# Unread matmuls in the gaps of the first attention steps, and three v loads split by rows

## The chip, the cores and the metric

The kernel runs on one core of a Trainium2 chip. Its time is the device time of one execution in microseconds (us). The timed runs are three; the profile is of one further execution. Engines are named as in the profile: PE (TensorE), PEld (its weight loads), DVE (VectorE), ACT (ScalarE), POOL (GpSimd) and SP, whose queue issues all the DMAs.

## The reference

Three stages follow each other. Attention over q, k, v of shape (2, 8, 576, 64), where a query sees only 32 keys: heads 0 to 3 the last 32 positions ("plain"), heads 4 to 7 every fourth of the last 128 ("dilated"). Then a layer with a softmax gate and a layer norm (512 to 1024 to 512). Then four experts, each 512 to 1024 with a ReLU and back, summed with the weights of each token.

```
masks = plain: 0 <= rel < 32;  dilated: 0 <= rel < 128 and rel % 4 == 0
attn  = softmax(where(mask, q @ k.T / 8, -1e9));  x = attn @ v
h     = x @ w_in;  solu = h * softmax(h);  x = layernorm(solu) * g @ w_out
out   = sum over e of p[:, e] * (relu(x @ w1[e]) @ w2[e])
```

Every output element depends on all of these. Nothing in the reference uses the products of the tile `warm`.

## The kernel before, in words

Attention is cut into 12 units: quad "P" (plain heads) and "D" (dilated heads), three tiles t each, for two batches b. A unit, `att_U`, has twelve steps: (1) score matmuls on PE, two that write the mask (line 256) and 24 small ones on q and k (line 265, 48 records in the profile); (2) the maximum on DVE (line 273); (3) subtraction on DVE (275); (4) exp on ACT (278); (5) sum (280) and (6) reciprocal (282) on DVE; (7) the product pd (284); (8) three transposes on PE (289); (9) copy to pt; (10) value matmuls on PE on pt and v (300); (11) copy to xhi; (12) the remainder xlo on DVE (238). PSUM tiles of the pool "pa" alternate between two buffers, so a unit's PE step can also wait for a DVE or ACT step of an earlier unit.

Beside it the weights of the first layer, in 64-bit floats, are converted: `conv_in` (VI.j) takes a loaded tile draw through ACT (lines 180, 182), DVE (184, 186), an addition (188), a copy to wh and a remainder wl (213). The first layer's matmuls `moe_H` (H.t, line 330) need the xhi and xlo of their tokens and wh and wl. Each matrix product is made of three products of high and low parts.

The order of all this is written out by hand in the string ORDER, one word per step: `UP.1.0` is the next step of unit P, t = 1, b = 0; `VI.2` the next of conversion 2; `lP`, `lD`, `lI`, `lvp`, `lvd`, `lO` issue a load; `F.n` calls `warm_up(n)`. A "+" chooses another engine for steps that have a choice. Each engine runs its share of that order strictly in sequence, and the SP queue issues loads in that order.

`warm_up(n)` issues n matmuls of 128x512 bf16 on a constant tile of ones into a PSUM tile that nobody reads. There are 16 in ORDER: `F.10` ahead of everything, then `F.2`, `F.1`, `F.1` and `F.2` between attention steps.

A load of v is one DMA of 128 rows of 3072 bytes: `load_vp(u, b)` takes a tile from a pool of two buffers, `load_vd(c, b)` fills a tile of its own. In SP's order of the opening, `lvp.0.0`, `lvd.1.0` and `lvd.0.0` come first, then `lP.0.1`, `lvp.1.0`, `lvp.2.0` (which takes the buffer that `lvp.0.0` filled, so it waits until unit P.0.0 has used it), `lI.3` (the draw load of conversion 3), `lD.1.1`, `lD.0.1`, `lvd.2.0`, and `lO.0.0`.

Of the kernel before, what the change touches and what calls it, by code (L numbers as in the profile page):

```python
# [23 lines left out]

ORDER = """
lP.0.0+ F.10 UP.0.0+ lI.0 lD.0.0 UD.0.0 UP.0.0 UP.0.0 VI.0 VI.0 VI.0+ VI.0+ UD.0.0+ UD.0.0 VI.0+ UP.0.0 UP.0.0 lI.4 VI.4+ VI.4 VI.4 VI.4+ VI.0 VI.4+ lD.1.0
UD.0.0 UD.0.0+ UD.0.0+ UD.0.0+ VI.4 F.2 UD.1.0 UD.1.0+ UP.0.0+ UP.0.0+ UD.1.0 lP.1.0+ VI.4+ VI.0+ F.1 UP.1.0 UP.1.0+ UD.1.0 UD.1.0 UD.1.0+ UD.1.0+ UP.1.0+
UP.1.0+ UD.2.0 UD.2.0 UD.2.0 UP.0.0 F.1 UP.2.0+ UP.0.0+ lI.1+ lI.2+ VI.1+ VI.1+ lO.0.1 VI.2+ UP.1.0+ UP.1.0+ UP.1.0+ UD.1.0 UD.1.0 UP.2.0+ UP.2.0+ VI.2
lvp.0.0 lvd.1.0 VI.1 F.2 UP.0.0 VI.1+ VI.1+ lvd.0.0 lP.0.1+ UP.0.0 UP.0.0+ UP.2.0+ UP.2.0+ UD.1.0 UD.1.0 UD.1.0+ VI.2 VI.2+ UD.0.0+ UD.0.0 VI.1 lvp.1.0 H.0+
UP.1.0+ VI.2+ lvp.2.0 VI.1 UP.0.1+ UP.1.0 UD.0.0 UP.0.1+ UP.0.1+ UP.2.0+ H.0 UD.2.0+ UD.2.0+ UD.2.0 UD.0.0 UD.0.0 lI.3 VI.3 UP.1.0+ UP.1.0 lD.1.1 UP.1.0  # L30
UD.2.0 VI.3+ VI.3 VI.3+ VI.2 H.1 VI.3 UD.2.0 lD.0.1 UD.0.1+ lvd.2.0+ UD.2.0 H.1+ UD.2.0+ VI.2 UD.0.1+ UD.0.1 UP.2.0+ VI.3 H.0 UP.0.1 UP.0.1+ UD.2.0 VI.3+
UD.2.0 UP.0.1+ UD.1.1+ UD.1.1 UD.1.1 lO.0.0+ UD.0.1+ VO.0.0 VO.0.0 VO.0.0+ endE+ VO.0.1+ H.0+ H.0 UP.2.0 UP.0.1+ UP.0.1+ UD.0.1 H.1+ VO.0.0 UP.2.0 UP.0.1 H.0+
H.0 lvp.0.1 UD.0.1 UP.2.0+ UP.2.0 UP.2.0 UP.0.1 UP.0.1+ H.1 UP.0.1 H.1+ UD.1.1+ UD.1.1 H.0+ T.0 VO.0.1 lvd.0.1+ VO.0.1 VO.0.1+ T.0 T.0 T.0 UD.2.1 UD.2.1+ misc
# [16 lines left out]
def fused_kernel(ctx, tc, qkp0, qkp1, qkd0, qkd1, vp, vd, w_in, w_out, gp, w1, w2, out):  # L50
    nc = tc.nc
# [51 lines left out]
    qkP, qkD, vdt = [], [], []  # L103
# [25 lines left out]
    rows = m0[:, 2, 1, 0:48]  # L129
# [9 lines left out]
    def load_qk(quad, t, b):  # L139
        dst, src = ((qkD, (qkd0, qkd1)), (qkP, (qkp0, qkp1)))[quad == "P"]  # L140
        nc.sync.dma_start(out=dst[b][t], in_=src[t][b])  # L141

    def load_vd(c, b):
        nc.sync.dma_start(out=vdt[b][c].rearrange("p m h d -> p (m h d)"), in_=vd[b, c])

    def load_vp(u, b):
        t = ap2.tile([128, 3, 4, D], F32, name="vp", tag="vp")
        vps[u, b] = t
        nc.sync.dma_start(out=t.rearrange("p m h d -> p (m h d)"), in_=vp[b, u])

    whi, wlo = {}, {}
    alt = [False]
# [461 lines left out]
    def load_misc():  # L614
# [4 lines left out]
              "VI": conv_in, "VO": conv_out, "H": moe_H, "T": moe_T, "X": moe_X, "WP": prep_w1, "XQ": prep_x,  # L619
              "WV": prep_w2, "u": lambda s: up(s, 0), "d": lambda t: down(0, t)}  # L620
    single = {"lD": lambda t, b: load_qk("D", t, b), "lP": lambda t, b: load_qk("P", t, b), "lvd": load_vd, "lvp": load_vp,
              "lI": load_in, "lO": load_out, "F": warm_up,
              "misc": load_misc, "endE": end_early, "endA": end_att, "endH": end_H, "lW": load_w1, "lV": load_w2, "endX": end_X, "sc": scales}
# [110 lines left out]
```

## Time and profile before

| | us |
|---|---|
| median of 3 runs | 531.86 (531.11 to 532.11) |
| profiled execution | 531.65 |
| its span | 529.9 |
| PE busy in the span | 519.2 (98%) |
| DVE busy | 347.7 (66%) |
| ACT busy | 192.1 (36%) |
| POOL busy | 179.8 (34%) |

The span runs from the first to the last instruction; what lies around it is the start and the end of the execution. An engine's busy time over the whole span says little about a stretch, so the rows below are read by stretches. The granted clock of PE has two levels here, 1.0 (2.4 GHz) and 0.5 (1.2 GHz). It is recorded only from 7.3 us on; what stands before that is an assumed 1.0. Some matmul records are missing from the trace, so a group's count can fall short (one unread matmul is shown at 20.01 us where the kernel has two).

### The profile page before, as it was taken

The page shows a single profiled execution, that of the slowest core. Times are in us where ns is not written, and L with a number is a line of the kernel's source. Part 1 is how long each engine was busy: PE and PEld are TensorE (multiplying, and loading weights), DVE is VectorE, ACT ScalarE, POOL GpSimd, SP SyncE. Part 2 cuts the span into 40 slices and gives each one's busy share as a digit, 9 for nine tenths or more (in the row PEclk, how much of TensorE's full clock was granted, in tenths as well). Part 3 has the DMA queues.
Part 4 walks back from the last instruction along what each step waited for, and adds up shares of the span by engine and source line. Part 5 has one row for each costly group of instructions (what it writes and reads, how often), then busy time and mean ns, then how long its engine had stood idle before and what let it go on. Part 6 is the DMA issues. An engine that isn't in the chain of part 4 may idle for free.

```text
span 529.9 us, 9444 instructions
## 1 busy us (share of the span) xinstructions
PE 519.2 (98%) x4020; PEld 464.3 (88%) x4024; DVE 347.7 (66%) x469; ACT 192.1 (36%) x296; POOL 179.8 (34%) x128
## 2 busy tenths in 40 slices
PE   6899999999999999999999999999999999999997
PEld 3677899889999998998989899898989889898986
DVE  6899994557789874855684485558448656853632
ACT  4778884353145142331422232143214213412210
POOL 3652231003403342730471173148117313820300
PEclk9799999999999999999999999999999999999999
DMA  8965330002042100400400040030004002000022
GB/s 320 392 255 188 119 117 2 0 1 80 1 160 95 65 2 6 155 0 1 145 15 1 0 160 1 0 126 34 2 1 159 1 1 79 1 0 1 2 79 99
DMA packets 15082, 37.98 MB, mean 72 GB/s; under 512 B 1344, under 2 KB 1600, under 8 KB 14656
## 3 DMA queue, kind: packets, MB, share of 16 engines
q1 hardware_dynamic: 15040, 37.38, 20.1%
q8 instruction: 31, 0.51, 0.4%
q14 instruction: 11, 0.09, 0.1%
HBM read 35.02 MB, written 2.36 MB: 71 GB/s over the span
## 4 chain that ended last, share of the span: by engine, by line
PE 95%; DMA 2%; DVE 2%; SPq 0%; issue 0%; ACT 0%; DVEq 0%
PE pa L564 19%; PE pm L564 18%; PE pm L492 17%; PE pa L492 17%; PE pm L379 10%; PE pm L330 9%; DMA qkP<-in_qkp_dram 2%; PE pa L300 2%; PE pa L358 2%; PE pa L265 1%; PE pa L289 1%; DVE st L273 0%; SPq L141 0%; PE pa L256 0%; ACT xhi L166 0%
## 5 line engine op out<-in xcount | busy, mean ns | idle before, releaser
L505 DVE SCALAR_TENSOR_TENSOR hl<-ct,hh 128x512 fp32r<-128x512 f32 (+1 forms) x64 | 63.0, 1005 | 34.8 <-ACT hh L503 34.7
L503 ACT ACTIVATE hh<-ct 128x512 fp32r<-128x512 f32 (+1 forms) x64 | 42.2, 682 | 59.2 <-DVE ct L523 23.9
L564 PE MATMUL pa<-wl,hh 128*128 128x512 f32 (+1 forms) x148 | 57.3, 387 | 0.0
L564 PE MATMUL pa<-wh,hh 128*128 128x512 f32 (+1 forms) x148 | 57.3, 387 | 0.0
L564 PE MATMUL pa<-wh,hl 128*128 128x512 f32 (+1 forms) x148 | 57.1, 386 | 0.0
L492 PE MATMUL pm<-xoh,hl 128*128 128x256 f32 (+1 forms) x192 | 56.8, 296 | 0.0
L492 PE MATMUL pa<-xoh,hl 128*128 128x256 f32 (+1 forms) x192 | 56.8, 296 | 0.0
L492 PE MATMUL pm<-xol,hh 128*128 128x256 f32 (+1 forms) x192 | 56.8, 296 | 0.0
L492 PE MATMUL pa<-xol,hh 128*128 128x256 f32 (+1 forms) x192 | 56.8, 296 | 0.0
L492 PE MATMUL pm<-xoh,hh 128*128 128x256 f32 (+1 forms) x192 | 56.8, 296 | 0.0
L492 PE MATMUL pa<-xoh,hh 128*128 128x256 f32 (+1 forms) x192 | 56.8, 296 | 0.0
L564 PE MATMUL pm<-wl,hh 128*128 128x512 f32 (+1 forms) x144 | 55.7, 387 | 0.0
L564 PE MATMUL pm<-wh,hh 128*128 128x512 f32 (+1 forms) x144 | 55.7, 387 | 0.0
L564 PE MATMUL pm<-wh,hl 128*128 128x512 f32 (+1 forms) x144 | 55.6, 386 | 0.0
L411 POOL TENSOR_TENSOR wl<-wl,wh 128x1024 fp32r<-128x1024 f32 x7 | 16.9, 2413 | 95.2 <-ACT wh L166 95.2
L569 DVE SCALAR_TENSOR_TENSOR xf<-pm,pr,xf 128x512 f32<-128x512 f32 (+1 forms) x32 | 23.6, 737 | 31.1 <-PE pm L564 31.1
L569 DVE SCALAR_TENSOR_TENSOR xf<-pa,pr,xf 128x512 f32<-128x512 f32 (+1 forms) x32 | 23.6, 738 | 30.4 <-PE pa L564 30.4
L411 POOL TENSOR_TENSOR hl<-sw,hh 128x512 fp32r<-128x512 f32 x20 | 29.8, 1488 | 37.8 <-ACT hh L166 24.0
L166 ACT CAST wh<-wl 128x1024 fp32r<-128x1024 f32 x16 | 16.8, 1052 | 70.8 <-PE pa L564 40.4
L492 PEld LDWEIGHTS pm<-xol,hh 128*128 128x128 f32 x192 | 36.4, 190 | 0.3
L492 PEld LDWEIGHTS pm<-xoh,hh 128*128 128x128 f32 x192 | 36.4, 190 | 0.3
L492 PEld LDWEIGHTS pa<-xoh,hh 128*128 128x128 f32 x192 | 36.4, 190 | 0.3
(197 smaller groups left out, 1243.4 us busy)
## 6 DMA issues: line engine op xcount, KB each, us to landing
wl<-in_moe_w_dram SPq DMA_DIRECT2D x16, 512.0 KB, 3.7
cvr<-in_moe_w_out_dram SPq DMA_DIRECT2D x8, 512.0 KB, 4.5
rw<-in_moe_w_dram SPq DMA_DIRECT2D x8, 512.0 KB, 5.8
wh<-in_moe_w_dram SPq DMA_DIRECT2D x8, 512.0 KB, 6.9
draw<-in_moe_w_in_dram SPq DMA_DIRECT2D x3, 1024.0 KB, 12.0
vp<-in_vp_dram SPq DMA_DIRECT2D x6, 384.0 KB, 6.0
vd<-in_vd_dram SPq DMA_DIRECT2D x6, 384.0 KB, 7.7
out_dram<-xf SPq DMA_DIRECT2D x8, 256.0 KB, 2.0
```

The costliest lines, as they stand in the source:

```text
L166: nc.scalar.copy(out, in_)
L265: nc.tensor.matmul(ps[32 * g:32 * g + 32, j, 64 * m:64 * m + 64], lhsT=qt[rows, h, xq:xq + 32], rhs=kt[rows, h, xq:xq + 64], start=False, ...
L300: nc.tensor.matmul(po[64 * (g % 2):64 * (g % 2) + 64, j, o:o + 32], lhsT=vt[rows, m, g, :], rhs=pt[rows, m, g, :], start=True, stop=True)
L330: nc.tensor.matmul(pm[:, n, :], lhsT=xx[:, kk, cols], rhs=ww["in", kk][:, 512 * n:512 * n + 512], start=(n_ == 0 and i < 2), stop=(n_ == K ...
L358: nc.tensor.transpose(pa[:, f // 4, (f % 4) * 128:(f % 4) * 128 + 128], e[:, f // 4, (f % 4) * 128:(f % 4) * 128 + 128], ident)
L379: nc.tensor.matmul(pm[:, dd, 0:CW], lhsT=w_, rhs=x_[:, f, :], start=(f == 0 and i == 0), stop=(f == KF - 1 and i == 2))
L411: pick().tensor_tensor(out=out, in0=a, in1=b, op=op)
L492: nc.tensor.matmul(ps[:, ff, 0:n], lhsT=a[:, kk, fc], rhs=b[:, kk, :], start=kk == 0 and m == 0, stop=kk == 1 and m == 2)
L503: nc.scalar.activation(out=hv, in_=src, func=AF.Relu)
L505: nc.vector.scalar_tensor_tensor(out=lv, in0=src, scalar=0.0, in1=hv.bitcast(F32), op0=ALU.max, op1=ALU.subtract)
L564: nc.tensor.matmul(po[:, 0, 0:dn], lhsT=h_[:, f, cols], rhs=w_, start=(f == 0 and i == 0), stop=(f == 3 and i == 2))
L569: nc.vector.scalar_tensor_tensor(out=acc[:, t, dc], in0=po[:, 0, 0:dn], scalar=pr[:, t, e:e + 1], in1=acc[:, t, dc], op0=ALU.mult, op1=ALU ...
```

## The change

Two things change. In ORDER the unread matmuls become 31: `F.2` is `F.9`, the first `F.1` is `F.4`, an `F.2` is added ahead of the first transposes of unit P.0.0 and an `F.3` ahead of the transposes of unit D.1.0; `F.10`, the second `F.1` and the last `F.2` stay. (The rest of the changed ORDER lines is a new line break.) And for batch 0 the loads of v for P tile 1, P tile 2 and D tile 2 are two DMAs each instead of one, of 120 and 8, 104 and 24, and 72 and 56 rows. The same bytes go to the same places.

```diff
--- before.py
+++ after.py
@@ -24,10 +24,10 @@
 
 ORDER = """
 lP.0.0+ F.10 UP.0.0+ lI.0 lD.0.0 UD.0.0 UP.0.0 UP.0.0 VI.0 VI.0 VI.0+ VI.0+ UD.0.0+ UD.0.0 VI.0+ UP.0.0 UP.0.0 lI.4 VI.4+ VI.4 VI.4 VI.4+ VI.0 VI.4+ lD.1.0
-UD.0.0 UD.0.0+ UD.0.0+ UD.0.0+ VI.4 F.2 UD.1.0 UD.1.0+ UP.0.0+ UP.0.0+ UD.1.0 lP.1.0+ VI.4+ VI.0+ F.1 UP.1.0 UP.1.0+ UD.1.0 UD.1.0 UD.1.0+ UD.1.0+ UP.1.0+
-UP.1.0+ UD.2.0 UD.2.0 UD.2.0 UP.0.0 F.1 UP.2.0+ UP.0.0+ lI.1+ lI.2+ VI.1+ VI.1+ lO.0.1 VI.2+ UP.1.0+ UP.1.0+ UP.1.0+ UD.1.0 UD.1.0 UP.2.0+ UP.2.0+ VI.2
-lvp.0.0 lvd.1.0 VI.1 F.2 UP.0.0 VI.1+ VI.1+ lvd.0.0 lP.0.1+ UP.0.0 UP.0.0+ UP.2.0+ UP.2.0+ UD.1.0 UD.1.0 UD.1.0+ VI.2 VI.2+ UD.0.0+ UD.0.0 VI.1 lvp.1.0 H.0+
-UP.1.0+ VI.2+ lvp.2.0 VI.1 UP.0.1+ UP.1.0 UD.0.0 UP.0.1+ UP.0.1+ UP.2.0+ H.0 UD.2.0+ UD.2.0+ UD.2.0 UD.0.0 UD.0.0 lI.3 VI.3 UP.1.0+ UP.1.0 lD.1.1 UP.1.0
+UD.0.0 UD.0.0+ UD.0.0+ UD.0.0+ VI.4 F.9 UD.1.0 UD.1.0+ UP.0.0+ UP.0.0+ UD.1.0 lP.1.0+ VI.4+ VI.0+ F.4 UP.1.0 UP.1.0+ UD.1.0 UD.1.0 UD.1.0+ UD.1.0+ UP.1.0+
+UP.1.0+ UD.2.0 UD.2.0 UD.2.0 F.2 UP.0.0 F.1 UP.2.0+ UP.0.0+ lI.1+ lI.2+ VI.1+ VI.1+ lO.0.1 VI.2+ UP.1.0+ UP.1.0+ UP.1.0+ F.3 UD.1.0 UD.1.0 UP.2.0+ UP.2.0+
+VI.2 lvp.0.0 lvd.1.0 VI.1 F.2 UP.0.0 VI.1+ VI.1+ lvd.0.0 lP.0.1+ UP.0.0 UP.0.0+ UP.2.0+ UP.2.0+ UD.1.0 UD.1.0 UD.1.0+ VI.2 VI.2+ UD.0.0+ UD.0.0 VI.1 lvp.1.0
+H.0+ UP.1.0+ VI.2+ lvp.2.0 VI.1 UP.0.1+ UP.1.0 UD.0.0 UP.0.1+ UP.0.1+ UP.2.0+ H.0 UD.2.0+ UD.2.0+ UD.2.0 UD.0.0 UD.0.0 lI.3 VI.3 UP.1.0+ UP.1.0 lD.1.1 UP.1.0
 UD.2.0 VI.3+ VI.3 VI.3+ VI.2 H.1 VI.3 UD.2.0 lD.0.1 UD.0.1+ lvd.2.0+ UD.2.0 H.1+ UD.2.0+ VI.2 UD.0.1+ UD.0.1 UP.2.0+ VI.3 H.0 UP.0.1 UP.0.1+ UD.2.0 VI.3+
 UD.2.0 UP.0.1+ UD.1.1+ UD.1.1 UD.1.1 lO.0.0+ UD.0.1+ VO.0.0 VO.0.0 VO.0.0+ endE+ VO.0.1+ H.0+ H.0 UP.2.0 UP.0.1+ UP.0.1+ UD.0.1 H.1+ VO.0.0 UP.2.0 UP.0.1 H.0+
 H.0 lvp.0.1 UD.0.1 UP.2.0+ UP.2.0 UP.2.0 UP.0.1 UP.0.1+ H.1 UP.0.1 H.1+ UD.1.1+ UD.1.1 H.0+ T.0 VO.0.1 lvd.0.1+ VO.0.1 VO.0.1+ T.0 T.0 T.0 UD.2.1 UD.2.1+ misc
@@ -140,13 +140,21 @@
         dst, src = ((qkD, (qkd0, qkd1)), (qkP, (qkp0, qkp1)))[quad == "P"]
         nc.sync.dma_start(out=dst[b][t], in_=src[t][b])
 
+    def rows(i, b):
+        p = {1: 120, 2: 104, 5: 72}.get(i, 128) if b == 0 else 128
+        return ((0, p), (p, 128))[:1 + (p < 128)]
+
     def load_vd(c, b):
-        nc.sync.dma_start(out=vdt[b][c].rearrange("p m h d -> p (m h d)"), in_=vd[b, c])
+        flat = vdt[b][c].rearrange("p m h d -> p (m h d)")
+        for p0, p1 in rows(3 + c, b):
+            nc.sync.dma_start(out=flat[p0:p1], in_=vd[b, c, p0:p1])
 
     def load_vp(u, b):
         t = ap2.tile([128, 3, 4, D], F32, name="vp", tag="vp")
         vps[u, b] = t
-        nc.sync.dma_start(out=t.rearrange("p m h d -> p (m h d)"), in_=vp[b, u])
+        flat = t.rearrange("p m h d -> p (m h d)")
+        for p0, p1 in rows(u, b):
+            nc.sync.dma_start(out=flat[p0:p1], in_=vp[b, u, p0:p1])
 
     whi, wlo = {}, {}
     alt = [False]
```

## Rows read from the trace of the kernel before

**Rows 1.** The page's slices: PE busy and granted clock, in tenths, 40 equal slices.
```profile
PE   6899999999999999999999999999999999999997
...
PEclk9799999999999999999999999999999999999999
```

**Rows 2.** Busy us (instructions) of PE, PEld, DVE, ACT, POOL; clock, DMA, GB/s.
```profile
7.30:10.70 3.40, 1.47 (x53) 0.87 (x52) 3.30 (x7) 1.74 (x3) 1.20 (x1) 1.00 1.01 417
10.70:21.00 10.30, 7.56 (x205) 5.01 (x208) 8.70 (x21) 6.70 (x10) 7.00 (x8) 0.50 1.01 408
21.00:32.00 11.00, 9.80 (x266) 7.82 (x267) 9.88 (x17) 8.35 (x14) 6.42 (x3) 1.00 1.00 385
32.00:60.00 28.00, 28.00 (x498) 22.16 (x496) 27.04 (x43) 22.33 (x37) 9.21 (x7) 1.00 0.50 171
```

**Rows 3.** PE in order of time: start us, us, work, idle before and releaser.
```profile
1.44 4.45 PE L79 MATMUL pm<-warm 128*128 128x512 bf16 x10 [1.44 <-DVE warm L74]
...
7.64 0.72 PE L265 MATMUL pa<-qkD 64*32 64x64 f32 x48
...
8.73 0.33 PE L256 MATMUL pa<-mask,identb 128*128 128x192 bf16 x2
11.20 0.97 PE L265 MATMUL pa<-qkD 64*32 64x64 f32 x48 [2.13 <-DMA qkD<-in_qkd_dram]
...
13.60 0.97 PE L265 MATMUL pa<-qkP 64*32 64x64 f32 x48 [0.58 <-DMA qkP<-in_qkp_dram]
...
16.44 0.87 PE L289 MATMUL pa<-ident,pd 128*128 128x128 f32 x3 [0.53 <-DVE sm L275]
17.53 0.53 PE L256 MATMUL pa<-mask,identb 128*128 128x192 bf16 x2 [0.22 <-DVE sm L275]
17.99 0.97 PE L265 MATMUL pa<-qkP 64*32 64x64 f32 x48
...
20.01 0.63 PE L79 MATMUL pm<-warm 128*128 128x512 bf16 x1 [0.22 <-issue]
21.16 0.90 PE L300 MATMUL pa<-pt,vp 64*64 64x32 f32 x48 [0.52 <-DMA vp<-in_vp_dram]
```

**Rows 4.** Tile vp: its DMA issues (ns, first and last start) and times to landing.
```profile
L149 SPq DMA_DIRECT2D vp<-in_vp_dram x6: 328/384/1247, 6.2 to 49.7; - x6
...
DMA to landing us min/median/max: 3.9/6.0/14.9
```

**Rows 5.** What PE waited for from 21 to 60 us: total, times, longest.
```profile
PE pm L330 <- ACT xhi L166: 0.6, 1, 0.6
PE pa L300 <- DMA vp<-in_vp_dram: 0.5, 1, 0.5
PE pa L289 <- DVE xlo L238: 0.2, 1, 0.2
PE pm L330 <- DVE wl L213: 0.2, 1, 0.2
```

**Rows 6.** DVE in order of time, 18 to 34 us.
```profile
19.00 0.56 DVE L273 TENSOR_REDUCE st<-pa 128x6 f32<-128x384 f32 x1 [0.40 <-PE pa L265]
...
20.85 1.23 DVE L186 SCALAR_TENSOR_TENSOR eva<-draw,eva 128x1024 uint32<-128x1024 uint32 x1
...
23.99 0.93 DVE L238 TENSOR_TENSOR xlo<-pa,xhi 128x192 fp32r<-128x192 f32 x2 [0.34 <-ACT xhi L166]
...
26.70 1.22 DVE L213 TENSOR_TENSOR wl<-eva,wh 128x1024 fp32r<-128x1024 f32 x1
```

**Rows 7.** ACT in order of time, 18 to 34 us.
```profile
28.51 1.17 ACT L180 ACTIVATE draw<-draw 128x1024 int32<-128x1024 uint32 x1 [0.44 <-DMA draw<-in_moe_w_in_dram]
30.06 0.48 ACT L166 CAST xhi<-pa 128x384 fp32r<-128x384 f32 x1 [0.39 <-PE pa L300]
```

**Rows 8.** SP's DMA issues, the vp load before the draw load, and two qkD.
```profile
22.11 0.33 SPq L149 DMA_DIRECT2D vp<-in_vp_dram  x1
...
22.96 1.44 SPq L141 DMA_DIRECT2D qkD<-in_qkd_dram  x1
```

## The prediction

> **What bounds the kernel now.** I read the slices first, then a table by stretches, then TensorE (PE), VectorE (DVE), ScalarE (ACT) and the SP queue instruction by instruction. The slices show PE full from the third slice to the end, at a granted clock of 1.0 [rows 1]. So there are two programs: an opening of some 32 us with waits and a slow clock, and a long rest that PE sets alone. The table sharpens that: from 32 to 60 us PE is busy 28.00 of 28.00; from 10.7 to 21.0 it is busy 7.56 of 10.30 us at a clock of 0.50, which is the 1.2 GHz level; from 21.0 to 32.0 it is busy 9.80 of 11.00 us, at 1.00 again [rows 2]. The change moves nothing behind the opening, so it can only bring PE to the same point of its program earlier or later. In the opening PE serves a chain that is mostly others' work, and the question is which wait ends last.
>
> That wait is at 21.16 us. The first value product (line 300, on pt and vp) starts there after 0.52 us of idle that a DMA of vp ended [rows 3]. That load was issued at 6.15 us (6.2 in its row, the first of its tile) and is the tile's longest, 14.9 us to landing: about 21.05 [rows 4]. From there on PE hardly waits: 0.6 us for ACT xhi, 0.2 for DVE xlo, 0.2 for DVE wl, besides the 0.5 just named [rows 5]. What happens before 21.05 is worth something only if it moves one of these. The page's chain of waits follows DVE back instead, and enters PE's second value product at about 22.1 from DVE line 186 (20.85 + 1.23 = 22.08) [rows 6]; but that product stands on PE behind the first, which runs 21.16 + 0.90 = 22.06 [rows 3], so a few hundredths hang on it.
>
> **The change, part by part.**
>
> *Nine unread matmuls instead of two, before the second D tile's scores.* At the lower level ten take 4.45 us, 0.43 to 0.44 each; the pair at 8.3 us fits between the end of the line-265 group (7.64 + 0.72 = 8.36) and the masks at 8.73, so about 0.2 each, half of it, as the 2.4 GHz level would give [rows 3]. Nine cost 9 x 0.215 = 1.9 us: 8.36 + 1.9 = 10.3, and the two mask matmuls 0.33 more, 10.6. The line-265 group behind them waited until 11.20 for qkD, after 2.13 us of idle [rows 3]. That idle hides them, with 0.6 us left. All at the lower level they would take 3.9 us and end with the masks at 12.8, and that group would be 1.6 us late.
>
> *Four instead of one, before the second P tile's scores.* If the clock is held, the qkD group takes 0.72 instead of 0.97 and ends at 11.92; 4 x 0.215 = 0.86 and masks 0.33 give 13.1, ahead of the qkP load that released the next group at 13.60 after 0.58 us of idle [rows 3]. Hidden again. At the lower level: 12.17 + 1.72 + 0.53 = 14.4, 0.8 us late.
>
> *The faster clock on what is there.* The P group of 13.60 ends 0.25 us earlier, and DVE's max follows it. The masks and the third P group, 17.53 to 18.96 [rows 3], take about 1.0 instead of 1.44 us, another 0.4; the DVE max that waited 0.40 us until 19.00 [rows 6] could begin about 18.4. So 0.65 us is won on this chain, line 186 ends near 21.4 instead of 22.08, and I expect the trace to show it.
>
> *Two more before the first transposes, three before the second ones.* 0.43 and 0.65 us. The first fall into the 0.53 us that PE idles there for DVE line 275 [rows 3]. The second push the second transposes: third P group done at 18.3, unread 18.95, transposes (three, about 0.55) 19.5, the old pair 0.43 to 19.9. Before, that pair ended at 20.01 + 0.63 = 20.64 [rows 3]. So PE reaches the first value product 0.7 us earlier and waits there until vp lands: 1.2 us of idle instead of 0.5.
>
> *What of that arrives after 21.16.* Nothing sizeable. vp's issue stands ahead of every split load in SP's queue, so its landing stays at 21.05 and the product at 21.16. DVE's xlo at 23.99 waits for ACT's copy of the second product (0.34 us of idle), and from there DVE runs without a hole through line 186 to line 213, 26.70 + 1.22 = 27.92 [rows 6], which ends PE's wait for wl [rows 5]. What DVE has done earlier does not bring these forward, since all of it stands behind xlo and xlo hangs on the product. The 0.6 us for xhi is ACT's copy after a later value product, 30.06 to 30.54 [rows 7], and stays. So the longer wait for vp swallows the 0.65 us. Bounds: nothing, to the 0.2 for wl won; I take 0.
>
> *The three split loads.* Three more DMA issues on SP. The first small part (8 rows) is issued before the vp load of 22.11, for which SP waited anyway [rows 8]: free. The second (24 rows) stands ahead of a draw load and two qkD loads, the third ahead of nothing urgent. An issue took from 0.33 us [rows 4] to 1.44 [rows 8]; I take 0.43, near the median of its line (0.38). The draw load then lands 0.43 later. ACT waited 0.44 us for it and started line 180 at 28.51 for 1.17 us [rows 7]; that would end at 30.11 instead of 29.68, against the xhi copy at 30.06 that PE waits for: 0.05 us. With 1.44: 31.12, so 1.06 us on PE. On the other side, a draw load that lands sooner takes away ACT idle that PE does not see: 0.
>
> [...]
>
> *Sum,* against the profiled execution (span 529.9, 1.75 around it, 531.65 in all, 0.21 under the median of the three runs): 0 + 0 + 0.05 = 531.7. Left at the profiled execution's own level, as a tenth is below what these terms can carry, I say 531.6.
>
> **Rivals.**
>
> *Faster: the clock of other executions.* In the profiled one the clock came back at 21.0, just ahead of the product at 21.16 [rows 2, 3]. If in other executions it comes back later, PE works at half rate where it sets the time, and loses up to half a microsecond per microsecond; 1 to 4 us later costs 0.5 to 2. The filled gaps would save that: 529.9 to 531.4. For it: the three runs spread over 1.0 us. Against: the profiled execution, with the clock back in time, is not below them.
>
> *Slower: the clock is not held and the added matmuls run at 0.43 us.* PE idled from about 9 to 11.20, and the clock was down from 10.7 [rows 2, 3]. If it falls in spite of the fill, PE itself gets late: the P group at 14.4 instead of 13.60 (0.8), two more unread 0.86 less the idle 0.53 (0.3), three more 1.29; 2.4 in all, less the 0.52 of wait at the first value product, 1.9: 533.5. It decides once PE reaches that product after 21.05, that is, from 0.52 us on. Half of it is likelier, as a PE so filled should get its clock back sooner than before. A form of the same: the new 1.2 us of idle ahead of 21.16 drops the clock just where PE sets the time; 2 to 4 us at the lower level cost up to 1 to 2. Against both: no idle is left as long as the 2.13 us that went with the fall.
>
> *Slower by the loads:* with the 1.44 us issue, 532.7; with one between, up to 532.2. Speaks for it that ACT already waits for that load; against it that only 0.38 us (30.06 - 29.68) separate a hidden delay from a seen one, but the usual issue is barely longer.
>
> *The clock is not held, and nothing is lost either:* the added matmuls stay in the gaps; 531.6, as forecast, by another way.
>
> **Numbers.** About 0.2% (1.06 us) is what a measurement of this kernel can tell from no change. No change, for either reason: 0.50, own range 531.0 to 532.3. The clock of other executions: 0.32, of which 0.22 beyond 0.2% and 0.10 within. Slower by the clock: 0.13, all beyond. Slower by the loads: 0.05, of which 0.03 beyond. That makes faster 0.22, within 0.62, slower 0.16. The range takes the nearer part of the faster case, 530.4 upward, and the smaller prices of the slower ones, to 532.8.
>
> **What would show it.** Right: a granted clock of 1.0 from 7.3 past 14 us; the P group of 13.60 in 0.72 us; the last unread matmul over by 20; the first value product still at about 21.16, with about 1.2 us of wait for vp; PE idle between 21 and 32 within 0.3 us of the 1.2 that it has now [rows 2]. Wrong: that product clearly before 21 or after 21.5, a clock that is down after 21, ACT's line 180 on the draw load later than 29, or a PE that still has holes after 32.

## The result, and the profile after

The changed kernel is slower. Its median is 536.56 us (535.68 to 537.97, 6 runs) against 531.95 us (531.11 to 532.28, 6 runs) for the kernel before: a ratio of 1.009, 95% interval 1.0074 to 1.0107. The forecast was 531.6, its range 530.4 to 532.8. The profiled execution took 536.16 us, with a span of 534.4; before it was 531.65 with 529.9. So 4.5 us of span are to be found. Lines of the changed kernel are numbered 8 higher than before from line 157 on (line 300 is 308, 330 is 338, 180 is 188, 166 is 174).

The page's slices of the changed kernel, to set beside [rows 1]:

```profile
PE   7779999999999999999999999999999999999997
...
PEclk9989999999999999999999999999999999999999
```

The loss is over after the third slice, some 40 us into the span; behind it PE is as full as it was. The table by stretches, beside [rows 2] (columns as there):

```profile
10.70:21.00 10.30, 6.81 (x213) 4.24 (x216) 8.81 (x21) 6.41 (x10) 7.01 (x8) 1.00 1.02 410
21.00:32.00 11.00, 8.43 (x260) 6.83 (x260) 8.20 (x14) 5.67 (x10) 6.38 (x3) 1.00 0.99 293
32.00:60.00 28.00, 26.07 (x434) 20.52 (x435) 23.99 (x39) 20.43 (x32) 8.65 (x7) 0.94 0.61 192
```

From 10.7 to 21.0 the unread matmuls do what they say: the clock is 1.00 where it was 0.50. From 21.0 on PE is busy for less (8.43 for 9.80, 26.07 for 28.00), and the last column points to a reason: from 21 to 32 us the DMA engines are as busy as before (0.99) and move 293 GB/s instead of 385.

PE in order of time, changed kernel (columns of [rows 3]):

```profile
14.14 0.72 PE L273 MATMUL pa<-qkP 64*32 64x64 f32 x48 [1.21 <-DMA qkP<-in_qkp_dram]
...
19.61 0.59 PE L79 MATMUL pm<-warm 128*128 128x512 bf16 x2
21.48 1.10 PE L308 MATMUL pa<-pt,vp 64*64 64x32 f32 x48 [1.28 <-DMA vp<-in_vp_dram]
...
29.67 0.90 PE L308 MATMUL pa<-pt,vp 64*64 64x32 f32 x48
33.83 0.74 PE L338 MATMUL pm<-wh,xhi 128*128 128x512 f32 x2 [3.26 <-ACT xhi L174]
34.41 0.92 PE L338 MATMUL pm<-wl,xhi 128*128 128x512 f32 x2
...
38.08 0.73 PE L338 MATMUL pm<-wh,xhi 128*128 128x512 f32 x2
```

and the three that answer to its last ones, in the kernel before:

```profile
29.09 0.90 PE L300 MATMUL pa<-pt,vp 64*64 64x32 f32 x48
30.59 0.73 PE L330 MATMUL pm<-wh,xhi 128*128 128x512 f32 x2 [0.60 <-ACT xhi L166]
...
33.33 0.73 PE L330 MATMUL pm<-wh,xhi 128*128 128x512 f32 x2
```

Set against each other they give PE's lag: 0.32 us at the first value product (21.48 against 21.16 in [rows 3]), 0.58 at the value product behind (29.67 - 29.09), 3.24 after the wait for xhi (33.83 - 30.59), 4.75 at the first-layer product that stood at 33.33 (now 38.08). Two steps make it, then. One idle of 3.26 us where 0.60 stood adds 2.66. And behind that idle the granted clock is 0.55 from 34.5 to 35.0 and 0.51 from 35 to 38, the lower level of [rows 2], and back at 1.00 from 38.0: another 1.51 us.

```profile
34.50:35.00 0.50, 0.50 (x3) 0.40 (x2) 0.48 (x2) 0.50 (x2) 0.00 (x0) 0.55 0.99 246
35.00:38.00 3.00, 2.91 (x56) 2.04 (x55) 2.93 (x4) 1.23 (x2) 0.00 (x0) 0.51 1.03 274
```

From there the two kernels run in step: PE's last matmuls are 4.7 us late, and the span is 4.5 us longer.

What ended that idle is ACT's copy, so ACT is read next, beside [rows 7]:

```profile
32.31 1.10 ACT L188 ACTIVATE draw<-draw 128x1024 int32<-128x1024 uint32 x1 [3.24 <-DMA draw<-in_moe_w_in_dram]
33.32 0.46 ACT L174 CAST xhi<-pa 128x384 fp32r<-128x384 f32 x1
```

ACT waited for the draw load until 32.29, 3.8 us later than before (28.49), and the xhi copy, behind it in ACT's order, came with it. On SP that load's issue moved far less. SP's own row in the changed kernel, and in the one before:

```profile
23.38 0.36 SPq L208 DMA_DIRECT2D draw<-in_moe_w_in_dram  x1
```

```profile
22.49 0.43 SPq L200 DMA_DIRECT2D draw<-in_moe_w_in_dram  x1
```

0.89 us of the 3.8 are a later issue. The other 2.9 are the load's own way: 8.9 us from issue to landing, 6.0 before. The stretch in which it is under way, in the kernel before and in the changed one:

```profile
22.00:28.00 6.00, 5.56 (x166) 4.38 (x161) 5.07 (x9) 4.76 (x9) 3.42 (x2) 1.00 0.99 372
```

```profile
22.00:28.00 6.00, 5.33 (x193) 4.42 (x188) 4.65 (x7) 4.03 (x8) 3.00 (x2) 1.00 0.99 234
```

Equal share, 372 against 234 GB/s: each packet takes longer. By the packets of the changed kernel's trace, in the median, one of 3072 bytes (a row of v) takes 125 ns from 10 to 21 us and 220 in these six microseconds, and one of 8192 bytes (the draw load, which isn't split) 313 and 540. So the split loads are slow here, and so is the whole load beside them.

### The profile page after: what moved, and what is told of

Read it like the earlier page. It is cut to its first block, busy times and chain, and to the rows that moved or that the text cites. A ratio compares the mean times of both kernels' runs of the same rounds, so it can differ in the third digit from the quotient of the medians.

```text
span 534.4 us, 9478 instructions
## 1 busy us (share of the span) xinstructions
PE 521.3 (98%) x4035; PEld 465.4 (87%) x4039; DVE 347.6 (65%) x469; ACT 192.0 (36%) x296; POOL 179.8 (34%) x128
## 4 chain that ended last, share of the span: by engine, by line
PE 92%; DMA 7%; SPq 0%; DVE 0%; issue 0%
PE pa L572 19%; PE pm L572 18%; PE pm L500 17%; PE pa L500 17%; PE pm L387 9%; PE pm L338 9%; DMA vd<-in_vd_dram 3%; DMA qkD<-in_qkd_dram 2%; PE pa L366 2%; DMA draw<-in_moe_w_in_dram 1%; PE pa L308 1%; PE pa L273 1%; PE pa L297 0%; SPq L141 0%; PE pa L264 0%; DVE xf L577 0%
## 5 line engine op out<-in xcount | busy, mean ns | idle before, releaser
L500 PEld LDWEIGHTS pa<-xol,hh 128*128 128x128 f32 x192 | 36.5, 190 | 0.3
```

The lines of the kernel that those rows point to most:

```text
L500: nc.tensor.matmul(ps[:, ff, 0:n], lhsT=a[:, kk, fc], rhs=b[:, kk, :], start=kk == 0 and m == 0, stop=kk == 1 and m == 2)
```

## The experiments

The main theory was that the split loads cost it all, by the rate at which they run. Its rivals: the added matmuls do it, alone or by the loads that they bring forward; the number of issues; too few DMA engines in use at 120, 104 and 72 rows; the order of the loads. Each ratio below is to runs of the kernel before that were taken together with that experiment, so its median differs a little from place to place (532.26 for e1 to e4, 532.68 for e5 to e8, 532.60 for e9 to e12).

**e1_fill: the unread matmuls alone.** The changed ORDER, loads whole; the edit is against the changed kernel, as in the next two.

```diff
-        for p0, p1 in rows(u, b):
-            nc.sync.dma_start(out=flat[p0:p1], in_=vp[b, u, p0:p1])
+        nc.sync.dma_start(out=t.rearrange("p m h d -> p (m h d)"), in_=vp[b, u])
... (load_vd in the same way)
```

> The 31 unread matmuls of the changed kernel, the loads of v in one piece as before. Theory A (the split loads alone cost the time: they bring down the rate of everything in flight, so the draw load lands 3.8 us late): 531.5 to 532.0, as before; ACT's start on that load at about 28.5, PE's wait for xhi at 0.6, the clock at 1.0 from 7.3 through the opening, and about 1.2 us of wait for vp ahead of the first value product at about 21.2. Rival B (more DMA issues and later issues): the same time. Rival C (the unread matmuls or the clock cost it): 534 or more.

532.45 us (531.67 to 534.14, 12 runs) against 532.26: 0.9993, 0.9975 to 1.0012. In its profile:

```profile
22.00:28.00 6.00, 5.69 (x182) 4.57 (x175) 4.82 (x7) 4.53 (x9) 2.58 (x2) 1.00 0.95 360
```

The rate is back (360 GB/s), the first value product stands at 21.32, the xhi wait is 0.60. The profile puts the product's idle of 1.69 us down to DVE line 186, which ended at 21.23, but the vp load too had landed only at 21.19. Within the interval the 15 added matmuls are worth nothing and cost nothing. One thing is new in this profile: PE stops for 0.83 us at 33.26, put down to "issue"; the last section comes back to such stops.

**e2_split: the split loads alone,** with the ORDER of before.

```diff
-UD.0.0 ... VI.4 F.9 UD.1.0 ... VI.0+ F.4 UP.1.0 ...
+UD.0.0 ... VI.4 F.2 UD.1.0 ... VI.0+ F.1 UP.1.0 ...
... (F.2 before UP.0.0 and F.3 before UD.1.0 left out)
```

> The three split loads (120+8, 104+24, 72+56), the 16 unread matmuls as before. Theory A: 536 to 537, the whole loss; 200 to 280 GB/s between 22 and 28 us; ACT waits 3 us or more for the draw load. Rival B: the same. Rival C: 532, the loss gone.

535.54 us (534.1 to 538.19, 10 runs): 1.0057, 1.0036 to 1.0079. ACT and the stretch in its profile:

```profile
30.54 1.16 ACT L188 ACTIVATE draw<-draw 128x1024 int32<-128x1024 uint32 x1 [1.21 <-DMA draw<-in_moe_w_in_dram]
```

```profile
22.00:28.00 6.00, 6.00 (x167) 5.27 (x165) 4.38 (x8) 4.05 (x8) 2.56 (x2) 0.72 0.85 252
```

The splits carry the loss, though the wait for the draw load is 1.21 us and not the 3 that were expected. They carry less of it without the fill: 1.0057 against 1.009, with intervals that overlap only from 1.0074 to 1.0079. The two ratios stand on different runs of the kernel before (medians 532.26 and 531.95); by their own medians the two kernels differ by 1.0 us. In this profile the clock was at 0.50 until about 25, the draw load was issued at 24.59 and took 5.9 us, since most of it ran after 27, when the rate was back at 399 GB/s. With the fill SP comes to it at 23.38, into slower traffic. That may be the difference; no run tests it.

**e3_split16: other row cuts,** 112+16, 96+32 and 64+64, all multiples of 16.

```diff
-        p = {1: 120, 2: 104, 5: 72}.get(i, 128) if b == 0 else 128
+        p = {1: 112, 2: 96, 5: 64}.get(i, 128) if b == 0 else 128
... (and the ORDER of before)
```

> The same three loads split at multiples of 16 rows: 112+16, 96+32, 64+64, with 16 unread matmuls. As many DMAs, issues and waits as in the split of the changed kernel. Theory A in the form 'which DMA engine writes which rows': any transfer that has not all 128 rows is laid on the engines in another way, so it stays slow, 534 to 537. Theory A in the form 'too few engines' (row counts that 16 does not divide): 531.5 to 533, with close to 390 GB/s between 22 and 28 us. Rival B: 536 to 537.

535.46 us (534.36 to 537.2, 10 runs): 1.0046, 1.0027 to 1.0065.

```profile
22.00:28.00 6.00, 5.68 (x167) 4.42 (x160) 5.24 (x9) 4.59 (x9) 3.38 (x2) 1.00 0.90 269
```

No better than e2 within the intervals, 269 GB/s. The form "too few engines" expected 531.5 to 533 and close to 390 GB/s of these cuts, and neither came; no trace here tells the engines apart.

**e4_cols and e5_cols_fill: the same number of DMAs, cut by columns** (all 128 rows, 720+48, 624+144 and 432+336 of 768 floats), without and with the fill; the edit is e4's, against the kernel before; e5 has the same on the changed kernel.

```diff
+        p = {1: 720, 2: 624, 5: 432}.get(i, 768) if b == 0 else 768
...
+            nc.sync.dma_start(out=flat[:, p0:p1], in_=vp[b, u, :, p0:p1])
```

> The same three loads split by columns instead of rows (720+48, 624+144, 432+336 of 768 values), each piece with all 128 rows, 16 unread matmuls. The same bytes in each piece as in the changed kernel, and as many DMAs, issues and waits. Theory A: close to the time before, 531.8 to 533 (shorter runs, one issue more ahead of the draw load, 0.4 us), with 350 to 400 GB/s between 24 and 28 us. Rival B: 536 to 537, since the issues are the same.

> The changed kernel with its 31 unread matmuls, and the three loads split by columns (720+48, 624+144, 432+336 values, 128 rows each) instead of by rows. Theory A (rows laid on the engines in another way slow the traffic): 531.8 to 533, since no row is moved and the clock is held; packets at their usual time between 22 and 28 us. Rival B (issues and waits of the queue): 535 to 537, as the changed kernel.

e4: 533.52 us (10 runs), 1.0021, 1.0000 to 1.0042. e5: 533.64 (10 runs), 1.0015, 0.9998 to 1.0032. Two stretches of e4:

```profile
22.00:28.00 6.00, 5.73 (x105) 5.21 (x106) 3.23 (x7) 3.14 (x6) 2.39 (x1) 0.51 0.70 220
28.00:32.00 4.00, 4.00 (x109) 3.15 (x107) 3.91 (x8) 2.10 (x4) 2.99 (x1) 0.88 1.00 387
```

The 220 looks like the row cut, but the share column says otherwise: the DMA engines were busy 0.70 of the time, as the second P load of v waits for the buffer that the first value product frees, and that product came at 22.27 and took 1.51 us, at a granted clock of 0.51 (22 to 28 us). The packets of the cut loads keep their speed: one of 2880 bytes takes 114 ns in the median, and in e5 the microsecond from 22 to 23, mostly theirs, has 371 GB/s at a share of 0.97. The 387 from 28 to 32 are whole loads behind them. So the extra issues and small pieces cost about 0.2%, with intervals from nothing to 0.4; the rest of the 0.9% needs the cut by rows. That a rate must be read with its share is the lesson of this pair.

How a cut by columns can cost shows in e5's profile, of the slowest of its runs: the draw load took 7.1 us to land, at a DMA share of 0.87 from 22 to 28 us, and PE waited 1.75 us for xhi.

```profile
30.61 1.13 ACT L188 ACTIVATE draw<-draw 128x1024 int32<-128x1024 uint32 x1 [2.01 <-DMA draw<-in_moe_w_in_dram]
```

So a late draw load is by itself no mark of the cut by rows; the longer packets are.

**e6_draw_first: the changed kernel with the draw load issued ahead of the split ones** (`lI.3` before `lvp.1.0`).

```diff
-... UD.0.0+ UD.0.0 VI.1 lvp.1.0
+... UD.0.0+ UD.0.0 VI.1 lI.3 lvp.1.0
... (lI.3 taken out of its old place)
```

> The changed kernel, its split loads kept, but the draw load of conversion 3 issued ahead of the first of them instead of behind the second. Theory A says that the loss is paid where ACT, in sequence, waits for that load: it then lands near 26 us, ACT's 3.2 us of wait and PE's 3.3 us of wait for xhi go (0.6 stays), and what is left is the lateness of the qkD load behind: 532 to 534. If the slow transfers cost PE in some other way (its operands, the other engines' access), the time stays at 536 to 537.

537.05 us (535.48 to 538.9, 5 runs), 1.0083, 1.0054 to 1.0112: nothing is won back, where 532 to 534 were expected if the loss were paid at the draw load alone. ACT indeed no longer waits for the load, and the xhi wait is 0.60 again. But PE:

```profile
29.50 0.41 PE L273 MATMUL pa<-qkP 64*32 64x64 f32 x19 [2.50 <-issue]
33.75 0.73 PE L338 MATMUL pm<-wh,xhi 128*128 128x512 f32 x2 [0.60 <-ACT xhi L174]
36.48 0.55 PE L297 MATMUL pa<-ident,pd 128*128 128x128 f32 x3 [1.07 <-issue]
38.45 0.85 PE L273 MATMUL pa<-qkD 64*32 64x64 f32 x48 [1.26 <-DMA qkD<-in_qkd_dram]
```

PE stops within one group of 48 matmuls, after 29 of them, for 2.50 us in which it waited for nothing that the profile shows. The changed kernel has the same break, 29 and 19, with 0.18 us. In the trace, a packet of 16 KB of the queue that the page calls "instruction" was under way from 26.77 and took 1.30 us, and PE went on 1.4 us after that packet's end. That PE waited there for its program is a guess from these times; no run shows it. Ahead of line 273 it waits another 1.26 us for a qkD load. The draw load was the first victim of the slow stretch, not its only one.

**e7_first_two and e9_third: parts of the splits,** with the fill.

```diff
-        p = {1: 120, 2: 104, 5: 72}.get(i, 128) if b == 0 else 128
+        p = {1: 120, 2: 104}.get(i, 128) if b == 0 else 128     # e7_first_two
+        p = {5: 72}.get(i, 128) if b == 0 else 128              # e9_third
```

> The changed kernel with two of the three splits (120+8 and 104+24), the third load whole. Theory A: these two stand ahead of the draw load, so nearly the whole loss, 535 to 536.5. If each split cost alike (rival B, one issue each): two thirds, 534.5 to 535.

> The changed kernel with the third split alone (72+56 of the D tile 2 load), the other two loads whole. Theory A: it stands behind the draw load and the two qkD loads in the queue, whose rate before it is untouched, and nothing that PE waits for comes soon behind it, so 532 to 533, at most half a microsecond over the kernel before. Rival B (each split costs alike): a third of the loss, 533.5 to 534.5.

e7: 536.06 us (533.26 to 536.93, 10 runs), 1.0054, 1.0034 to 1.0074. e9: 533.64 (532.37 to 535.02, 10 runs), 1.0017, 1.0000 to 1.0034. ACT in e7, then in e9:

```profile
32.54 1.13 ACT L188 ACTIVATE draw<-draw 128x1024 int32<-128x1024 uint32 x1 [3.52 <-DMA draw<-in_moe_w_in_dram]
```

```profile
29.18 1.17 ACT L188 ACTIVATE draw<-draw 128x1024 int32<-128x1024 uint32 x1 [0.56 <-DMA draw<-in_moe_w_in_dram]
```

The two splits ahead of the draw load do most of it: e7 lies where the main theory had it (535 to 536.5), above two thirds of the loss (534.5 to 535). The one behind costs little, but e9 doesn't decide by itself: its 533.64 is above the 532 to 533 expected and inside the 533.5 to 534.5 of equal costs, with an interval from nothing to 0.34%.

**e8_rates and e10_rates2: the rate of a row cut by itself.** Both are the kernel before with the later loads of w2 (two of 512 KB in each step g) cut by rows, at a time when PE is full and little else is in flight but the loads of w1 issued behind them. Each ran once, for its rates; its time (533.96 and 533.12 us) says nothing here.

```diff
+            p = {3: 120, 4: 104, 5: 72, 6: 112, 7: 64}.get(g, 128)              # e8_rates
...
+            cuts = {3: (0, 64), 4: (0, 32, 64, 96), 5: tuple(range(0, 128, 16)), 7: (0, 96)}.get(g, (0,))   # e10_rates2
+            if g == 6: parts = [slice(0, 128, 2), slice(1, 128, 2)]
```

> The kernel before, its v loads whole; instead the loads of the second layer's w2 slices, which come two at a time (512 KB each, 128 rows of 2 x 2 KB) in the long stretch where PE sets the time and no other loads run, are split by rows, another way in each group g: 3: 120+8, 4: 104+24, 5: 72+56, 6: 112+16, 7: 64+64; 1 and 2 whole. This measures the rate by itself. Theory A, form 'which engine writes which rows': all of groups 3 to 7 are slower than 1 and 2, by 1.3 to 2 times in time to landing, 64+64 no better than 120+8. [...] Rival B: all alike, but for 0.4 us per issue. The whole time is as before, 532 to 533, if these loads are off the path.

> The loads of the w2 slices once more, off the path, cut by rows: group 3: 64+64, 4: four of 32, 5: eight of 16, 6: even rows and odd rows (64 each), 7: 96+32; 1 and 2 whole. [...] Form 'fewer rows in a transfer, slower': four of 32 clearly under 64+64, and even and odd rows equal to 64+64. Form 'few engines': 64+64, four of 32 and eight of 16 at the full rate of 370 to 400.

e8, by single microseconds: whole loads at 173 to 175, 120+8 rows at 262 to 266, 104+24 at 310 to 312:

```profile
173.00:174.00 1.00, 1.00 (x6) 0.85 (x5) 0.99 (x2) 0.00 (x0) 0.00 (x0) 1.00 1.02 367
174.00:175.00 1.00, 1.00 (x6) 0.81 (x6) 1.00 (x3) 0.00 (x0) 0.00 (x0) 1.00 1.01 377
...
262.00:263.00 1.00, 1.00 (x9) 1.00 (x8) 1.00 (x2) 0.00 (x0) 0.00 (x0) 1.00 1.00 225
263.00:264.00 1.00, 1.00 (x9) 1.00 (x9) 0.76 (x2) 0.15 (x1) 0.00 (x0) 1.00 1.02 203
264.00:265.00 1.00, 1.00 (x9) 1.00 (x8) 0.52 (x1) 1.00 (x3) 0.46 (x1) 1.00 0.98 209
265.00:266.00 1.00, 1.00 (x9) 1.00 (x8) 0.31 (x1) 1.00 (x3) 1.00 (x2) 1.00 1.06 227
...
310.00:311.00 1.00, 1.00 (x9) 1.00 (x8) 0.67 (x2) 0.24 (x1) 0.00 (x0) 1.00 1.09 201
311.00:312.00 1.00, 1.00 (x9) 1.00 (x8) 0.60 (x1) 1.00 (x3) 0.54 (x1) 1.00 0.99 221
```

At a share near 1.0 these rows have 367 to 377 GB/s for whole loads and 201 to 227 for the same bytes cut by rows. That overstates the difference, since the whole rows are late ones of their group. Its first full microsecond, also of whole loads, is no faster than a cut:

```profile
170.00:171.00 1.00, 1.00 (x7) 0.91 (x7) 1.00 (x2) 0.98 (x2) 0.00 (x0) 1.00 1.00 201
```

A steadier measure is the time of a packet. In each group the first 512 packets of 2048 bytes (1 MB) are, by SP's order, those of the w2 loads:

| w2 loads | median packet, ns | first MB, us |
|---|---|---|
| whole (two groups of e8) | 84, 84 | 4.5, 4.4 |
| 120+8 | 139 | 5.2 |
| 104+24 | 146 | 5.3 |
| 72+56 | 84, a quarter above 124 | 4.8 |
| 112+16 | 92 | 3.9 |
| 64+64 (e8, e10) | 133, 136 | 4.8, 4.6 |
| 96+32 (e10) | 108 | 4.7 |
| even, odd rows (e10) | 84 | 4.4 |

So a cut by rows by itself lengthens packets, unevenly: 120+8 and 104+24 by two thirds and three quarters, 112+16 hardly. Nothing of the opening is needed for it. It was expected that all cuts in e8 would be slower by 1.3 to 2 times; in time for the first MB the slowest is 1.2 times the whole.

e10 asked which property of the cut does it, and answers in part. 64+64 rows:

```profile
263.00:264.00 1.00, 1.00 (x9) 1.00 (x8) 0.35 (x1) 0.99 (x2) 0.30 (x1) 1.00 1.02 252
264.00:265.00 1.00, 1.00 (x9) 1.00 (x8) 0.47 (x1) 1.00 (x3) 1.00 (x2) 1.00 1.08 229
```

Around these, 64+64 runs at 199 to 268 GB/s, 96+32 at 252 and 258. Even and odd rows run at 182 to 369; the 369 are their own, as the whole loads behind them were issued only in that microsecond. They have as many DMAs and rows in each as 64+64, and keep the whole load's packet time. So the number of DMAs or of rows isn't what lengthens the packets; which rows stand together matters. Cuts in four fall to 115 GB/s at a share of 0.52 and to 166 at 1.00, and cuts in eight at about 0.55 are bound by their issues, one per 0.46 us; I read no rate from these two.

What it is in a row cut that costs the rate stays open.

**e11_early_fill and e12_early: a better order, with whole loads.** The draw load and both qkD loads ahead of the vp load that waits for its buffer, and one 512 KB load (`lO.0.1`) put behind; e11 with the fill, e12 without.

```diff
-... H.0+ UP.1.0+ VI.2+ lvp.2.0 VI.1 ... lI.3 VI.3 ... lD.1.1 ... lD.0.1 ...
+... H.0+ UP.1.0+ VI.2+ lI.3 lD.0.1 lD.1.1 lvp.2.0 VI.1 ... VI.3 ... lvd.2.0+ lO.0.1 ...
```

> A version that may beat both: 31 unread matmuls, loads whole, and the queue reordered: the w_out load that is read only after 40 us goes behind the third vd load, and the draw load of conversion 3 and the two qkD loads go ahead of the vp load that waits for its buffer. vp then lands about 1.3 us earlier, the first value product starts near 20.0 instead of 21.2, and ACT doesn't wait for the draw load: 530.3 to 531.5, ratio 0.996 to 0.999 to the kernel before, if the theory is right that the opening is set by landings; 532 if something else sets it.

> The same reordered queue with the 16 unread matmuls of the kernel before. If holding the clock is worth nothing, as the run with the 31 alone suggests, the same time as with 31. If the earlier landing needs the faster chain ahead of it (the old chain reaches the value product at 20.64 at the earliest), 0.4 to 0.8 us more.

e11: 534.0 us (533.11 to 534.81, 12 runs), 1.0015, 1.0000 to 1.0031. e12: 532.52 (531.53 to 533.27, 12 runs), 0.9987, 0.997 to 1.0003. In e11 the first value product comes at 20.13, and ACT no longer waits for the draw load. What is won is lost on PE, in e11 and in e12:

```profile
27.22 0.41 PE L265 MATMUL pa<-qkP 64*32 64x64 f32 x19 [1.75 <-issue]
```

```profile
27.38 0.30 PE L265 MATMUL pa<-qkP 64*32 64x64 f32 x4 [0.89 <-issue]
```

In e11 the clock falls to 0.61 from 28 to 32 besides. Expected were 530.3 to 531.5 for e11, and for e12 the same time or up to 0.8 us more; it took 1.5 us less. So with this order the fill seems to cost time, and no version beats the kernel before by more than its interval.

## Why the prediction was wrong, step by step

**Right: the unread matmuls.** All the signs named for them came: the clock at 1.00 from 10.7 to 21.0, the P group of 13.60 in 0.72 us (though at 14.14, for its qkP load), the unread matmuls over at 20.2, 1.28 us of wait for vp (1.2 was forecast), the value product at 21.48 (21.16). Less came on DVE: line 186 ended at 21.81, 0.26 us earlier and not 0.65. e1 puts their worth at 0.9993. By their starts in the changed kernel's trace they follow each other every 0.216 us at the granted clock of 1.00, the ten ahead of 7.3 us every 0.427: 2.4 and 1.2 of the 512 columns per ns. No trace here has the clock in GHz; where the text before the result gives it so, these rates are what was measured. The rival "clock not held" fell with the same rows.

**Right in place, wrong in size: the three split loads.** The step that failed is this term: "An issue took from 0.33 us [rows 4] to 1.44 [rows 8]; I take 0.43 [...] The draw load then lands 0.43 later", hence 0.05 us on PE. The path named there (draw load, ACT line 180, the xhi copy, PE) is the path of the loss. Of the load's 3.80 us, 3.26 came through to the copy (30.06 to 33.32), so 0.54 was hidden where 0.38 was forecast. But the load landed 3.8 us later: 0.89 by its issue, 2.9 by the rate. The term priced a DMA by its issue alone and carried "the same bytes" over at the rate of before; in the stretch with the split loads the DMA engines moved 234 GB/s instead of 372 at the same share, with e8's cut packets (139 and 146 ns for 84) showing that the cut does this by itself. And with the DMA engines full from 7.3 to 32 us ([rows 2]: shares of 1.00 and 1.01), a lower rate is a later landing for all that is queued. The view that should have set a wider range was there: the share column said that this resource had nothing to spare, and none of the rows that I read was of a load cut by rows. The term's upper bound of 1.06 us came from an issue, so it was no bound. Three of the signs of being wrong came with it: line 180 on the draw load at 32.31, later than 29; PE with holes after 32 (busy 26.07 of 28.00); a clock down after 21.

**Missed: what an idle costs behind itself.** I weighed a fall of the clock for the 1.2 us ahead of the value product, where it did not come (clock 1.00 from 21 to 32). It came behind the 3.26 us, and cost 1.51.

**The rivals.** "Slower by the loads", with 532.7, had the true path, though by a long issue and not by the rate, at a chance of 0.05 and under a fifth of its price (0.8 instead of 4.6 us over the median before). "The clock of other executions" exists: in the profile of e8, whose opening is that of before, the clock was 0.50 in each microsecond from 21 to 27. Yet with the clock held in e1 the time was the same within the interval (0.9975 to 1.0012).

**Open.** Why cutting by rows lowers the rate, and why 112+16 hardly does so in e8, while e3, with 96+32 and 64+64 beside it, lost as much as e2; whether fill and splits together cost more than apart (1.009 against 1.0057 and 0.9993), and why; whether the stalls put down to "issue" are PE's program arriving late.

## What to carry to other kernels

When a change cuts or reshapes a DMA, look at the share column where it runs: at a share of 1.0 (here 234 GB/s for 372, from 22 to 28 us) price it by rate, for itself and for every load queued with it, and take no rate over from a load of another shape; the time of a packet was a steadier measure here (84 ns in both whole groups of e8, with single microseconds from 201 to 377 GB/s near full share) than the rate of one microsecond. As far as these runs go, keep loads at their full 128 rows; if one must be cut, the cut by columns cost some 0.2% here (not clear of nothing), the three cuts by rows 0.5 to 0.9%. And filling PE's gaps gained nothing here (e1: 0.9993, 0.9975 to 1.0012), where the next thing that PE waited for was a landing.

## What the runs showed of the hardware

- A whole load beside split ones is slow too: its 8192-byte packets took 540 ns in the median instead of 313. In e6 the same load's packets took 313 to 320 ns until 24 us, ahead of the split ones, and the 6656-byte packets of the qkD load behind took 396 to 524 instead of 253.
- PE stopped inside a group of equal matmuls for 2.50 (e6), 1.75 (e11) and 0.89 us (e12), each time while loads filled the DMA engines (shares of 1.04, 1.01 and 1.02 from 22 to 28 us), and e11 and e12 have no split load. The page counts 31 packets with 0.51 MB for the "instruction" queue of the changed kernel, about 16 KB each. That the stalls are waits for these packets was not shown.
- Two things in the traces speak for such a wait, without proving it. All eight stops put down to "issue" after 25 us in the traces of this case (changed kernel, e1, e2, two in e6, e8, e11, e12) stand ahead of the 477th, 604th or 731st pair of weight load and matmul in PE's program, 127 apart, with the 15 added matmuls or without: hence 29 matmuls of the group ahead of the stop in e11 and 44 in e12. And each ended 1.2 to 1.5 us after a 16 KB packet of the instruction queue did.
- In the changed kernel the granted clock was 0.55 and then 0.51 from 34.5 to 38.0 us, behind PE's 3.26 us of idle; behind the 1.28 us ahead of the value product it stayed at 1.00. The length of the idle doesn't decide it alone: behind the 1.75 us in e11 the clock fell (0.61 from 28 to 32), behind the 2.50 us in e6 it was 1.00 in that stretch.
